# Moving tiles of a feed-forward stage read from the last column to the first, its weight words interleaved

## The chip, the cores and the metric

The kernel runs on one core of one Trainium2 chip. The metric is the device time of one execution in microseconds. Before the change it is 3116.07 us, the median of three runs (3114.22 to 3117.28).

## The reference

Two blocks stand one behind the other, all in float32. The first is a long convolution: a small network makes a filter of 12480 positions by 128 channels, and `u = x * v` (4 batches) is convolved with it by a Fourier transform of twice the length, then multiplied by `x`. The second is a feed-forward block on the 49920 tokens that come out of it:

```
u = x * v
y = np.fft.irfft(np.fft.rfft(u, n=L, axis=1) * Hf, n=L, axis=1)[:, :S, :]
x = (x * y).reshape(B * S, 128)
h = np.maximum(x @ w_in, 0.0)        # w_in: 128 x 2048
out = h * h @ w_out                  # w_out: 2048 x 128
```

## The kernel before

**The feed-forward part.** The tokens are cut into 98 column tiles (two of 446 columns, 50 of 512 and 46 of 510; `GN`). For each tile `i` and each of 8 pairs of hidden blocks `f`, `m_h` multiplies two 128x128 blocks of `w_in` with the tokens, `m_g` takes relu and square on ScalarE and VectorE, `m_l` makes the low word on VectorE, and `m_o` multiplies two 128x128 blocks of `w_out` with the result and adds it up over `f` in one PSUM bank. Every operand is kept as two float32r words, a high and a low one, and `mm3` makes one product of three matmuls: high weights by high moving tile (L95), low weights by the same high tile (L96), high weights by the low tile (L97). So one `f` is 12 matmuls, each with a weight load of its own, and the whole part has 98 x 8 x 12 = 9408 of them. Their moving operands are the tiles `zh`, `zl` (tokens) and `gh`, `gl` (hidden values).

**Where these tiles lie.** A weight tile `wt` holds 256 columns of both words, 2048 bytes in a partition: before, all 256 high words and then all 256 low words, so that the 128 words of one load are next to each other. The pools are filled from both ends of SBUF. Before, `zh`, `zl`, `gh` and `gl` of the pool `mp` begin at the same remainder of their address by 512 as the weight tiles (480). Once the convolution is done, `m_g` uses a second pool (`tp`, the name `tail`) for odd `f`; its tiles begin at remainder 128.

**The convolution** runs through four stages for each batch: `stage1` (L290 to L293), `stage2` (L380), `stage3` (L492) and `stage4`, whose matmuls are again three float32r ones by `mm3` (moving `ah`, `al` of 256 columns, stationary `tb` of 112). The other stages use plain float32 matmuls. In `stage3` the weights are every second word of the tile `v` (a step of 8 bytes). The order of all work is written out by hand: generators yield at three points, and the feed-forward loop calls `adv` to run the next piece of the next batch's convolution between its own matmuls. When all batches are through, the feed-forward part runs alone to the end.

Of the kernel before, what the change touches and what calls it, by code (L numbers as in the profile page):

```python
# [7 lines left out]
F32 = mybir.dt.float32  # L8
F32R = mybir.dt.float32r
# [8 lines left out]
I = 112  # L18
# [9 lines left out]
NS = NF // 2  # L28
# [10 lines left out]
TH = 4  # L39
CW = 256  # L40
NCW = DFF // CW


@with_exitstack
def hyena_moe_kernel(
# [34 lines left out]
    def pool(name, side="left", **kw):  # L80
        return tc.tile_pool(name=name, bufs=kw.pop("bufs", 2), side=side, reuse_waits="tile", **kw)
# [7 lines left out]
        for _ in range(k):  # L89
            nc.tensor.matmul(o[:, :128], zeros, zeros, start=True, stop=True)  # L90

    def mm3(o, L, R, first=True, last=True):
        lh, ll = L
        rh, rl = R
        nc.tensor.matmul(o, lh, rh, start=first, stop=False)  # L95
        nc.tensor.matmul(o, ll, rh, start=False, stop=False)  # L96
        nc.tensor.matmul(o, lh, rl, start=False, stop=last)  # L97
# [10 lines left out]
    def convert_weights(p, wp, raws, wt, chunks):  # L108
        V = nc.vector
        for c in chunks:  # L110
            low, high = raws[c][:, :, 0], raws[c][:, :, 1]
            mag, top, sgn = (p.tile([128, CW], I32, tag=k, name="cv") for k in ("cm", "ct", "cs"))
            mf = mag.bitcast(F32)
            tf = top.bitcast(F32)
            V.tensor_scalar(out=top, in0=high, scalar1=0x7FFFFFFF, scalar2=None, op0=ALU.bitwise_and)
            yield
            V.tensor_scalar(out=mf, in0=tf, scalar1=2.0**-15, scalar2=122880.0, op0=ALU.max, op1=ALU.min)
            yield
            V.tensor_scalar(out=top, in0=mag, scalar1=3, scalar2=0x7FFFFFFF, op0=ALU.logical_shift_left, op1=ALU.bitwise_and)
            yield  # L120
            V.tensor_scalar(out=mag, in0=low, scalar1=1, scalar2=None, op0=ALU.logical_shift_right)
            nc.gpsimd.tensor_copy(mf, mag)
            yield
            V.tensor_scalar(out=sgn, in0=high, scalar1=-0x80000000, scalar2=0x40000000, op0=ALU.bitwise_and, op1=ALU.bitwise_xor)
            yield
            V.tensor_tensor(out=top, in0=top, in1=sgn, op=ALU.bitwise_xor)
            wt[c] = wp.tile([128, 2, CW], F32R, tag="w", name="wt", bufs=2 * NCW)
            hi12, lo12 = wt[c][:, 0, :], wt[c][:, 1, :]
            nc.gpsimd.tensor_copy(hi12, tf)
            yield  # L130
            V.tensor_scalar(out=sgn, in0=top, scalar1=-0x800000, scalar2=None, op0=ALU.bitwise_and)
            yield
            V.scalar_tensor_tensor(out=mf, in0=mf, scalar=2.0**-51, in1=sgn.bitcast(F32), op0=ALU.mult, op1=ALU.mult)
            yield
            V.tensor_sub(out=tf, in0=tf, in1=hi12.bitcast(F32))
            yield
            V.tensor_add(out=lo12, in0=tf, in1=mf)
            yield
# [386 lines left out]
    def stage4(b, done, ring=None):  # L525
# [21 lines left out]
        with pool("s4") as p:  # L547
# [22 lines left out]
            def mm(t):  # L570
                if t >= NP:
                    return
                hi, lo = q.pop(t)
                tb = L.pop(t)
                A = bank()
                o = A[:I, :256]
                mm3(o, (tb[:, 0, :], tb[:, 2, :]), (hi[:, 0], lo[:, 0]), last=False)
                mm3(o, (tb[:, 1, :], tb[:, 3, :]), (hi[:, 1], lo[:, 1]), first=False)
                Y[t] = A

            def turn_first(t):

                zf = p.tile([I, 2 * D], F32, tag="zf", name="zf", bufs=1)
                nc.vector.tensor_mul(
                    out=zf.rearrange("p (c b i) -> p b c i", b=4, c=2),
                    in0=Y.pop(t)[:I, :256].rearrange("p (b i c) -> p b c i", b=4, c=2),
                    in1=X.pop(t).rearrange("p (b c i) -> p b c i", b=4, c=2),
                )
                o = bank()
                for c in range(2):  # L590
                    nc.tensor.transpose(o[:, c * I : (c + 1) * I], zf[:, c * D : (c + 1) * D], ident)
                idle(2)
                return o[:, 1 : 2 * I]
# [9 lines left out]
            def out_t(t):  # L603
                if t not in Y:
                    return
                xv = X.pop(t).rearrange("p (b c i) -> p b c i", b=4, c=2)
                zt = Z[t // 2 % 2]
                nc.vector.tensor_mul(
                    out=zt[:I].rearrange("p (b t c i) -> p t b c i", b=4, t=2, c=2)[:, t % 2],
                    in0=Y.pop(t)[:I, :256].rearrange("p (b i c) -> p b c i", b=4, c=2),  # L610
                    in1=xv,
                )
                if t % 2 == 0:
                    return
                zs = p.tile([128, 4 * D], F32, tag="zs", name="zs")
                nc.vector.transpose(out=zs, in_=zt)
                for k, w in enumerate(GW):
                    dst = zpart(b, t // 2, k).rearrange("(i b w) -> i b w", i=32, b=4)
                    src = zs[32 * k : 32 * k + 32]
                    if k == 0:  # L620
                        dst = dst.rearrange("i b (t w) -> i (b t) w", t=2)
                        src = src.rearrange("p (b t w) -> p (b t) w", b=4, t=2)[:, :, 1:]
                    elif k == 3:
                        dst = dst.rearrange("i b (q w) -> i (b q) w", q=4)
                        src = src.rearrange("p (b q w) -> p (b q) w", b=4, q=4)[:, :, :16]
                    else:
                        src = src.rearrange("p (b w) -> p b w", b=4)
                    nc.sync.dma_start(out=dst, in_=src)
                done[b] = t + 1
# [107 lines left out]
    wt = {}  # L737
# [13 lines left out]
    idle(20)  # L751
    held["tbb"].close()

    mp = ctx.enter_context(pool("mp", "right"))
    head = [mp.tile([D, GM], F32R, tag=k, name=k)[:, :GT] for k in ("zh", "zl")]
    s4 = stage4(0, done, take("t1p"))
# [1 line left out]
    idle(12)  # L758

    def wi(k, h, f):  # L760
        return wt[k * NCW + f // 2][:, h, f % 2 * 128 : (f % 2 + 1) * 128]

    def zload(i):
        zi = mp.tile([D, GM], F32, tag="zi", name="zi", bufs=1)[:, : GN[i]]
# [20 lines left out]
    def m_h(zT, f):  # L785
        A = psa.tile([128, 2, 512], F32, tag="A", name="A")
        for t in range(2):
            mm3(A[:, t, : zT[0].shape[1]], (wi(0, 0, 2 * f + t), wi(0, 1, 2 * f + t)), zT)
        return A

    def m_g(A, p, n, between, way):
# [31 lines left out]
    def m_o(i, f, hl):  # L823
        if f == 0:
            O[0] = bank() if tail and not nxt[0] else pso.tile([128, 512], F32, tag="O", name="O")
        o = O[0][:, : GN[i]]
        for t in range(2):
            mm3(o, (wi(1, 0, 2 * f + t), wi(1, 1, 2 * f + t)), (hl[0][:, t, :], hl[1][:, t, :]), first=(f == 0 and t == 0), last=(f == NS - 1 and t == 1))
        if f == NS - 1:
            return i, o  # L830
        return None

    def m_out(last):
        if last is not None:
            i, o = last
            ot = mp.tile([D, GM], F32, tag="ot", name="ot", bufs=1)[:, : GN[i]]
            nc.scalar.copy(ot, o)
            nc.sync.dma_start(out=out[:, GO[i] : GO[i] + GN[i]], in_=ot)
# [32 lines left out]
    for i in range(NM):  # L871
        for f in range(NS):
            adv(1)
            A = m_h(zT, f)
            last = m_o(*pend.pop(0)) if len(pend) > 1 else None
            adv(2)
            if not nxt[0] and not tail:
                tail.append(ctx.enter_context(pool("tp")))
            late.append((i, f, m_g(A, tail[0] if tail and f % 2 else mp, GN[i], lambda: m_out(last), way(i * NS + f))))
            while len(late) > len(tail):  # L880
                x, y, st = late.pop(0)
                pend.append((x, y, m_l(st, False)))
            if i + 1 < NM:
                if f == (1 if i else 3):
                    ready(i + 1)
                    zi = zload(i + 1)
                if f == (4 if i else 6):
                    nzT = zsplit(zi)
            adv(3)
            n = i * NS + f  # L890
            if stage[0] != since[0]:
                since = stage[0], n + 4
            owed += EXTRA[done[1] > 0]
            if owed >= 1 and stage[0] in (("s3", "s4") if done[1] else ("s2", "s3", "s4")) and nxt[0] == 1 and n >= since[1]:
                owed -= 1
                since = stage[0], n + 3
                for k in range(1, 4):
                    adv(k)
        if i + 1 < NM:
            zT = nzT  # L900
# [116 lines left out]
```

## Time and profile before

| what | value |
|---|---|
| median of three runs | 3116.07 us (3114.22 to 3117.28) |
| the profiled execution: span | 3112.0 us |
| TensorE matmul busy | 3072.7 us, 99% of the span |
| TensorE weight load busy | 2579.8 us, 83% |
| VectorE busy | 2538.0 us, 82% |
| ScalarE busy | 2419.1 us, 78% |
| GpSimd busy | 1501.6 us, 48% |

The span runs from the first to the last instruction of one profiled execution; the runs are timed without the profiler, around the whole execution, and their median stands 4.1 us above it. Matmuls are pipelined: the busy time of one contains the time in which its last columns leave the array, so that two successive ones overlap in the table. The pace is read from start to start.

### The profile page before, as it was taken

What the parts mean: (1) busy time and instruction counts of PE and PEld (TensorE: products, weight loads), DVE (VectorE), ACT (ScalarE), POOL (GpSimd) and SP (SyncE); (2) the same over time, 40 slices, a digit from 0 to 9 for tenths busy, and PEclk for the clock granted to TensorE, in tenths of its full rate; (3) what the DMA queues carried; (4) which work ended last, traced back from release to release, by engine and by line L of the source; (5) the groups of instructions that cost most, each with busy time, mean ns of one, the idle gap of its engine ahead of it and who ended that gap; (6) DMA issues with size and microseconds to landing.
All of it is one profiled execution on the core that took longest, in us unless ns stands there. A gap on an engine that the chain in (4) does not pass through costs nothing.

```text
span 3112.0 us, 49107 instructions
## 1 busy us (share of the span) xinstructions
PE 3072.7 (99%) x16086; PEld 2579.8 (83%) x16086; DVE 2538.0 (82%) x3080; ACT 2419.1 (78%) x3130; POOL 1501.6 (48%) x1631
## 2 busy tenths in 40 slices
PE   9989999999999999999999999999999999999999
PEld 7767888888888888888888888888888888888887
DVE  7888898878877988878877898878877799777776
ACT  5556777777788777788888877787788887878787
POOL 1249765556544565546644575646644466000000
PEclk9999999999999999999999999999999999999999
DMA  5783574434200664434300375434410176100000
GB/s 184 263 294 99 137 166 137 124 111 145 67 21 15 151 161 132 130 91 127 115 15 21 80 176 144 133 92 121 124 51 14 36 168 156 33 24 24 24 26 20
DMA packets 342623, 323.11 MB, mean 104 GB/s; under 512 B 161968, under 2 KB 288800, under 8 KB 342368
## 3 DMA queue, kind: packets, MB, share of 16 engines
q1 hardware_dynamic: 313216, 272.25, 30.2%
q0 software_dynamic: 29152, 47.72, 6.4%
q8 instruction: 128, 2.10, 0.3%
q14 instruction: 127, 1.04, 0.1%
HBM read 231.78 MB, written 65.60 MB: 96 GB/s over the span
## 4 chain that ended last, share of the span: by engine, by line
PE 92%; POOL 2%; DMA 2%; DVE 2%; issue 1%; ACT 1%; SPq 0%; DVEq 0%; ACTq 0%; POOLq 0%
PE A L95 11%; PE A L97 11%; PE A L96 11%; PE O L97 9%; PE O L96 9%; PE O L95 9%; PE F L380 6%; PE F L492 6%; PE F L293 5%; PE F L97 4%; PE F L95 4%; PE F L96 4%; PE A L290 2%; PE A L291 1%; POOL W L405 1%
## 5 line engine op out<-in xcount | busy, mean ns | idle before, releaser
L799 ACT ACTIVATE r<-A 128x1024 f32<-128x1024 f32 (+2 forms) x784 | 803.8, 1025 | 420.8 <-PE A L97 407.0
L818 DVE TENSOR_TENSOR gl<-r,gh 128x1020 fp32r<-128x1020 f32 (+1 forms) x433 | 642.5, 1484 | 113.9 <-ACT r L806 80.0
L95 PE MATMUL A<-zh,wt 128*128 128x512 f32 (+2 forms) x1568 | 671.4, 428 | 0.9 <-DVE gl L818 0.9
L97 PE MATMUL A<-zl,wt 128*128 128x512 f32 (+2 forms) x1568 | 613.8, 391 | 0.0
L96 PE MATMUL A<-zh,wt 128*128 128x512 f32 (+2 forms) x1568 | 612.9, 391 | 0.0
L802 ACT ACTIVATE gh<-r 128x1024 fp32r<-128x1024 f32 (+2 forms) x461 | 486.9, 1056 | 62.8 <-PE O L96 57.2
L97 PE MATMUL O<-gl,wt 128*128 128x512 f32 (+2 forms) x1248 | 487.4, 391 | 4.2 <-DVE gl L818 4.2
L96 PE MATMUL O<-gh,wt 128*128 128x512 f32 (+2 forms) x1248 | 485.0, 389 | 0.0
L95 PE MATMUL O<-gh,wt 128*128 128x512 f32 (+2 forms) x1248 | 484.9, 389 | 0.0
L804 DVE SCALAR_TENSOR_TENSOR A<-A,r 128x1024 f32<-128x1024 f32 (+2 forms) x350 | 425.4, 1215 | 68.1 <-ACT r L799 66.5
L818 DVE TENSOR_TENSOR gl<-A,gh 128x1024 fp32r<-128x1024 f32 (+2 forms) x350 | 426.1, 1218 | 63.1 <-ACT gh L802 20.4
L806 ACT ACTIVATE r<-r 128x1020 f32<-128x1020 f32 (+1 forms) x434 | 460.3, 1061 | 12.5
L813 DVE CAST gh<-r 128x1020 fp32r<-128x1020 f32 (+1 forms) x323 | 225.6, 698 | 221.2 <-ACT r L806 152.7
L782 POOL TENSOR_TENSOR zl<-zi,zh 128x512 fp32r<-128x512 f32 (+2 forms) x97 | 126.4, 1303 | 522.4 <-ACT zh L781 506.1
L567 POOL TENSOR_TENSOR al<-W,ah 112x512 fp32r<-112x512 f32 x214 | 281.9, 1318 | 189.2 <-ACT ah L561 185.0
L501 POOL TENSOR_TENSOR W<-c 112x224 f32<-112x224 f32 x256 | 217.6, 861 | 285.7 <-ACT c L499 275.0
L97 PEld LDWEIGHTS A<-zl,wt 128*128 128x128 f32 x1568 | 294.6, 188 | 64.7
L95 PEld LDWEIGHTS A<-zh,wt 128*128 128x128 f32 x1568 | 295.5, 188 | 51.4 <-DVE gl L818 3.1
L96 PEld LDWEIGHTS A<-zh,wt 128*128 128x128 f32 x1568 | 296.2, 189 | 45.1
L417 POOL TENSOR_TENSOR W<-W,m 112x256 f32<-112x256 f32 x168 | 177.8, 1058 | 247.3 <-DVE m L415 233.1
L97 PEld LDWEIGHTS O<-gl,wt 128*128 128x128 f32 x1248 | 234.2, 188 | 54.5 <-DVE gl L818 5.9
L96 PEld LDWEIGHTS O<-gh,wt 128*128 128x128 f32 x1248 | 234.2, 188 | 50.6
(127 smaller groups left out, 5495.3 us busy)
## 6 DMA issues: line engine op xcount, KB each, us to landing
ht<-Hd SPq DMA_DIRECT2D x224, 256.0 KB
tb<-t POOLq DMA_DIRECT2D x224, 196.0 KB, 3.1
xt<-x SPq DMA_DIRECT2D x224, 112.0 KB
xt<-xs SPq DMA_DIRECT2D x96, 224.0 KB
vt<-vs SPq DMA_DIRECT2D x96, 224.0 KB
tb<-t2s SPq DMA_DIRECT2D x168, 112.0 KB
Hd<-he SPq DMA_DIRECT2D x28, 512.0 KB
zd<-zs SPq DMA_DIRECT2D x222, 64.0 KB
```

What stands on the lines that cost most here:

```text
L95: nc.tensor.matmul(o, lh, rh, start=first, stop=False)
L96: nc.tensor.matmul(o, ll, rh, start=False, stop=False)
L97: nc.tensor.matmul(o, lh, rl, start=False, stop=last)
L380: nc.tensor.matmul(U[:I, k * 256 : (k + 1) * 256], tb[:KP, k, :], a[:, k], start=True, stop=True)
L501: nc.gpsimd.tensor_sub(out=dst[:, 1], in0=c[:, :, 0:3:2], in1=c[:, :, 3:0:-2])
L567: eng.tensor_sub(out=lo, in0=w, in1=hi.bitcast(F32))
L799: nc.scalar.activation(r, h, AF.Relu)
L802: nc.scalar.activation(hi, r, AF.Square)
L804: nc.vector.scalar_tensor_tensor(out=h, in0=h, scalar=0.0, in1=r, op0=ALU.max, op1=ALU.mult)
L806: nc.scalar.activation(r, r, AF.Square)
L813: nc.vector.tensor_copy(hi, g)
L818: nc.vector.tensor_sub(out=lo, in0=g, in1=hi.bitcast(F32))
```

## The change

Three things change, and no instruction moves: on each of the five queues the same instructions stand in the same order on the same operands' shapes. Buffers have other addresses, and four instructions (three of L799, one of L818) wait for other transfers, since a tile lies on other earlier tiles.

1. `mm3` gets a flag `back`, with which it reads both words of the moving tile from the last column to the first. The two calls of the feed-forward part and the two of `stage4` set it. In the feed-forward part the hidden values come out reversed and are reversed again by the second product, so the output has its old order; in `stage4` the VectorE multiplication that reads the PSUM bank (L584, L608) reads it from the end.
2. A weight tile holds high and low word of one column side by side: the 128 words of one load now stand 8 bytes apart, over 1024 bytes.
3. Two unused tiles, of 128 bytes (`gp`) ahead of the pool `mp` and of 224 bytes (`tp`) in the tail's pool, shift the tiles behind them. All of `zh`, `zl`, `gh`, `gl`, in either pool, now begin at remainder 352 by 512, and the weight tiles as before at 480.

```diff
+TP = 56
+MP = 32
...
-    def mm3(o, L, R, first=True, last=True):
+    def mm3(o, L, R, first=True, last=True, back=False):
         lh, ll = L
-        rh, rl = R
+        rh, rl = (x[:, ::-1] for x in R) if back else R
...
-            wt[c] = wp.tile([128, 2, CW], F32R, tag="w", name="wt", bufs=2 * NCW)
-            hi12, lo12 = wt[c][:, 0, :], wt[c][:, 1, :]
+            wt[c] = wp.tile([128, CW, 2], F32R, tag="w", name="wt", bufs=2 * NCW)
+            hi12, lo12 = wt[c][:, :, 0], wt[c][:, :, 1]
...
-                mm3(o, (tb[:, 0, :], tb[:, 2, :]), (hi[:, 0], lo[:, 0]), last=False)
-                mm3(o, (tb[:, 1, :], tb[:, 3, :]), (hi[:, 1], lo[:, 1]), first=False)
+                words = [[x[:, a].rearrange("p d c -> p (d c)") for x in (hi, lo)] for a in range(2)]
+                mm3(o, (tb[:, 0, :], tb[:, 2, :]), words[0], last=False, back=True)
+                mm3(o, (tb[:, 1, :], tb[:, 3, :]), words[1], first=False, back=True)
...
-                    in0=Y.pop(t)[:I, :256].rearrange("p (b i c) -> p b c i", b=4, c=2),
+                    in0=Y.pop(t)[:I, 255::-1].rearrange("p (b i c) -> p b c i", b=4, c=2),
...
+    ctx.enter_context(pool("gp", "right")).tile([128, MP], F32, name="gp", bufs=1)
     mp = ctx.enter_context(pool("mp", "right"))
...
-        return wt[k * NCW + f // 2][:, h, f % 2 * 128 : (f % 2 + 1) * 128]
+        return wt[k * NCW + f // 2][:, f % 2 * 128 : (f % 2 + 1) * 128, h]
...
-            mm3(A[:, t, : zT[0].shape[1]], (wi(0, 0, 2 * f + t), wi(0, 1, 2 * f + t)), zT)
+            mm3(A[:, t, : zT[0].shape[1]], (wi(0, 0, 2 * f + t), wi(0, 1, 2 * f + t)), zT, back=True)
...
-            mm3(o, (wi(1, 0, 2 * f + t), wi(1, 1, 2 * f + t)), (hl[0][:, t, :], hl[1][:, t, :]), first=(f == 0 and t == 0), last=(f == NS - 1 and t == 1))
+            mm3(o, (wi(1, 0, 2 * f + t), wi(1, 1, 2 * f + t)), (hl[0][:, t, :], hl[1][:, t, :]), first=(f == 0 and t == 0), last=(f == NS - 1 and t == 1), back=True)
...
                 tail.append(ctx.enter_context(pool("tp")))
+                tail[0].tile([128, TP], F32, tag="tp", name="tp", bufs=1)
```

## Rows read from the trace of the kernel before

**Rows 1.** The page: span, busy time by engine, TensorE's granted clock in 40 slices.

```profile
span 3112.0 us, 49107 instructions
...
PE 3072.7 (99%) x16086; PEld 2579.8 (83%) x16086; DVE 2538.0 (82%) x3080; ACT 2419.1 (78%) x3130; POOL 1501.6 (48%) x1631
...
PEclk9999999999999999999999999999999999999999
```

**Rows 2.** The page: the chain that ended last, shares of the span by engine.

```profile
PE 92%; POOL 2%; DMA 2%; DVE 2%; issue 1%; ACT 1%; SPq 0%; DVEq 0%; ACTq 0%; POOLq 0%
```

**Rows 3.** Busy time by stretch: PE, PEld, DVE, ACT, POOL (instructions), clock, DMA share, GB/s.

```profile
1000.00:1200.00 200.00, 198.79 (x1041) 168.73 (x1040) 178.81 (x208) 157.74 (x188) 108.20 (x125) 1.00 0.59 141
...
2700.00:2800.00 100.00, 100.00 (x439) 82.07 (x438) 74.03 (x74) 79.61 (x82) 6.47 (x5) 1.00 0.09 24
```

**Rows 4.** Timeline of the tail: start us, length us, engine, line, operation.

```profile
2900.59 0.40 PE L95 MATMUL F<-gh,wt 128*128 128x510 f32 x1
2900.59 0.19 PEld L96 LDWEIGHTS F<-gh,wt 128*128 128x128 f32 x1
...
2901.99 0.39 PE L95 MATMUL A<-zh,wt 128*128 128x510 f32 x1
...
2903.36 0.39 PE L95 MATMUL F<-gh,wt 128*128 128x510 f32 x1
...
2904.72 0.39 PE L95 MATMUL A<-zh,wt 128*128 128x510 f32 x1
```

**Rows 5.** Groups of PE matmuls by form: count, busy us, mean ns, idle before.

```profile
L97 PE MATMUL A<-zl,wt 128*128 128x512 f32 x800 | 315.5, 394 | 0.0
L96 PE MATMUL A<-zh,wt 128*128 128x512 f32 x800 | 313.9, 392 | 0.0
L97 PE MATMUL O<-gl,wt 128*128 128x512 f32 x800 | 313.4, 392 | 4.2 <-DVE gl L818 4.2
...
L95 PE MATMUL O<-gh,wt 128*128 128x512 f32 x800 | 311.7, 390 | 0.0
...
L96 PE MATMUL A<-zh,wt 128*128 128x510 f32 x736 | 287.4, 390 | 0.0
...
L380 PE MATMUL F<-W,tb 120*112 120x256 f32 x672 | 170.2, 378 | 0.0
...
L95 PE MATMUL O<-gh,wt 128*128 128x510 f32 x416 | 161.5, 388 | 0.0
...
L95 PE MATMUL F<-ah,tb 112*112 112x256 f32 x448 | 125.4, 280 | 0.4 <-ACT ah L561 0.4
...
L97 PE MATMUL F<-gl,wt 128*128 128x510 f32 x320 | 125.4, 392 | 0.0
...
L96 PE MATMUL A<-zh,wt 128*128 128x446 f32 x32 | 11.6, 364 | 0.0
```

**Rows 6.** A piece of the chain in order of time: start us, length us, what.

```profile
659.91 1.73 PE F L380 x8
```

**Rows 7.** Groups of weight loads by form: count, busy us, mean ns, idle before.

```profile
L96 PEld LDWEIGHTS A<-zh,wt 128*128 128x128 f32 x1568 | 296.2, 189 | 45.1
...
L492 PEld LDWEIGHTS F<-ft,v 112*112 112x112 f32 x1792 | 209.0, 182 | 19.0 <-POOL v L479 5.3 <-DVE W L500 1.1
...
L380 PEld LDWEIGHTS F<-W,tb 120*112 120x112 f32 x672 | 117.8, 175 | 29.5
```

**Rows 8.** The tile `wt`: ns min/median/max of one group, first and last start us.

```profile
L129 POOL CAST wt<-cv x16: 466/522/524, 88.9 to 151.0; 128x256 fp32r<-128x256 f32 x16
```

**Rows 9.** Groups of VectorE's instructions: count, busy us, mean ns, idle before.

```profile
L608 DVE TENSOR_TENSOR z<-F,xt 112x256 f32<-112x256 f32 x222 | 90.5, 410 | 7.2 <-DMA xt<-x 7.2
...
L137 DVE TENSOR_TENSOR wt<-cv 128x256 fp32r<-128x256 f32 x16 | 6.8, 424 | 0.5
...
L117 DVE TENSOR_SCALAR cv<-cv 128x256 f32<-128x256 f32 x16 | 4.7, 294 | 0.6
...
L115 DVE TENSOR_SCALAR cv<-raw 128x256 int32<-128x256 int32 x16 | 4.6, 286 | 0.0
```

More of the change, by code (lines that the diff above doesn't have):

```diff
@@ L609, in out_t @@
                     out=zt[:I].rearrange("p (b t c i) -> p t b c i", b=4, t=2, c=2)[:, t % 2],
-                    in0=Y.pop(t)[:I, :256].rearrange("p (b i c) -> p b c i", b=4, c=2),
+                    in0=Y.pop(t)[:I, 255::-1].rearrange("p (b i c) -> p b c i", b=4, c=2),
                     in1=xv,
```

## The prediction

> **What bounds the kernel now.** The page comes first. TensorE is busy for 99% of the span, the others for 48 to 83%, and the granted clock is at nine tenths or more in every slice [rows 1], that is, at 2.4 GHz, the higher of its two levels, nearly throughout. The chain that ended last is TensorE for 92% [rows 2]. So what a matmul costs is what the kernel costs, and the question is whether a matmul takes longer than its columns need.
>
> The table by stretch gives the pace. Between 2700 and 2800 us the feed-forward part runs alone: 439 matmuls of 510 columns in 100 us, 227.8 ns from start to start, with no gap [rows 3]. At 2.4 GHz 510 columns, one in each clock, are 212.5 ns, so 15.3 ns go elsewhere. A matmul of the same kernel that loses almost nothing is that of `stage2`: 8 follow each other in 1.73 us, 216.3 ns each [rows 6], for 256 columns. It is plain float32, two clocks to a column, so 512 clocks or 213.3 ns, and only 3 ns more. The two differ by some 12.4 ns (216.3 less two clocks is 215.4). The groups by form say the same of the whole run: 378 ns for the 512 clocks of L380, against 390 to 394 ns for the 512 clocks of L95 to L97 [rows 5].
>
> The timeline of the tail shows that this surplus hangs on where the tile lies. Six matmuls from `gh` and `gl`, of one shape, with weights from the same tiles, take 1.40 us (2900.59 to 2901.99) and some microseconds later 1.36 us (2903.36 to 2904.72) [rows 4]. The two sixes differ in the pool from which `gh` and `gl` come: the first has odd `f` (the tail's pool, remainder 128), the second even `f` (remainder 480, as the weights). The rows also show what runs beside a matmul: the weight load of the next one starts with it (2900.59 both) and lasts 0.19 us. I read the surplus as stalls in which the moving read and the weight read want the same part of SBUF. That is an inference: the trace shows that the cost depends on the tile's place, not which part of the memory was asked for.
>
> Against this reading stands the Trainium skill, TensorE: Matmul & The Clock Gate, section "Step-by-step: what each phase is for": TensorE has two independent SBUF read ports, and loading the next weights takes nothing from the running matmul. By that rule there is nothing to gain, the term below is 0 and the time 3116 us. The 1.40 against 1.36 us do not fit it, but they alone do not name the weight load.
>
> **The change part by part.** *The meeting of the two reads.* A load of 128 columns takes 189 ns, one of 112 takes 175 [rows 7]: 14 ns for 16 columns, 0.88 ns or about two clocks a column; 128 columns are read in about 110 ns, the first half of a matmul. So before, the moving read goes 4 bytes on in each clock and the weight read 4 bytes in two clocks; they pass each other again and again. After, the weight words are 8 bytes apart, 4 bytes a clock on average: both walk at one pace. If the array takes its weights from the last column to the first (no row shows this), both also walk the same way, and keep the distance with which they begin; the moving tiles' remainder 352 and the weights' 480 set it to 128 bytes. Two reads at one pace cannot run into each other again once they are apart, so I expect nearly all of the surplus to go.
>
> Its size, by lengths against 378 ns for 512 clocks (377 for 510, 350 for 446) [rows 5]. L96 of the same form as a shown L95 lies within 2 ns, and L95 of `A`, whose mean holds the switch from float32 matmuls ahead of it, is taken as L96. 512 columns: 2400 into `A` at 393 ns, 15 over, 36.0 us; 2400 into `O` at 391, 13 over, 31.2. 510 columns: 2208 into `A` at 390, 13 over, 28.7; 1248 into `O` at 389, 12 over, 15.0; 960 into `F` at 392, 15 over, 14.4. 446 columns: 192 at 364, 14 over, 2.7. Together 128 us. By the pace of the tail it is 9408 x 12.4 = 117 us. I take 122 us, and leave a tenth of it, 12 us, to first meetings: **110 us gained**. Bounds: 128 us gained, and, with stalls doubled because weight reads now touch twice the memory, 122 us lost.
>
> *`stage4`.* 1344 matmuls of 256 columns, 280 ns at 378 - 256 / 2.4 = 271 [rows 5], 9 over: 12 us in all. Only the direction changes here; the weights stay 4 bytes apart, so the paces still differ. Between 12 us gained and 12 lost, I take **6 us gained**, since reads that walk the same way meet less often.
>
> *Loads from every second word.* L492 loads every second word already: 182 ns for 112 columns against 175 for L380's adjacent ones [rows 7]. With 7 ns more the new load takes 196 ns and is hidden under the matmul of 215 ns. Twice the reading time would not be hidden (189 + 110 = 299 ns a matmul, 9408 x 71 = 670 us more), but L492 is far from that. I take 0.
>
> *Reading a tile backwards.* No row of TensorE has a negative step, so its own price is not shown; the pace of two clocks a column of L380 [rows 5, 6] would be its worst, and nothing its best. I take nothing: the same words are read, in the other order. VectorE's 222 instructions of L608 [rows 9] read their bank backwards at the same distance of two words as before. I take 0 there too; 10% more would be 9 us, hidden on an engine that is busy for 82% [rows 1].
>
> *Writing the weights.* 16 casts of 522 ns on GpSimd [rows 8] and 16 results of 424 ns on VectorE [rows 9] now write every second word. Twice as long would be 15 us, around 90 to 155 us and partly on the path. Reading every second word costs VectorE nothing: L115 does in 286 ns what L117 does from adjacent words in 294 [rows 9]. I take 0 by this, and the range has room for the other end.
>
> *What is late next.* With TensorE some 4 to 5% faster, VectorE rises from 178.81 of 200 us to about 94% between 1000 and 1200 us [rows 3], a `stage4` stretch; those last about 600 us in all. It remains below 100%, but the queues are in order and TensorE will wait for `gl` now and then (4.2 us in all before, at L97 [rows 5]). 4% of 600 us is 24 us between nothing and all given back; I take half, **12 us lost**. In the tail VectorE (74%) and ScalarE (80%) have room [rows 3].
>
> Sum: 110 + 6 - 12 = 104 us. The profiled span is 3112.0 us, which gives 3008, and the median stands 4.1 us above the span: **3012 us**.
>
> **The rivals.** *Some of the surplus stays* (14 in 100). The distance of 128 bytes is not enough, or part of the surplus is no stall but belongs to the float32r form: between the two sixes lie only 6 ns a matmul, not 12. Half of the 122 us gained gives 3055; by how much stays, 3046 to 3100 and a little above.
>
> *Nothing happens* (7 in 100). The whole surplus belongs to float32r, and only the tail's odd tiles gain what the even ones have: some 640 matmuls at 6 ns, 4 us, 3112. This is also what the rule of the Trainium skill's TensorE page, cited above, would lead to.
>
> *The reads meet more* (16 in 100). If the array takes its weights from the first column on, both reads walked the same way before, 2 bytes apart in a clock; the reversed moving read would now come towards the weight read, 8 bytes in a clock, over weights of 1024 bytes instead of 512. For it speaks that no row tells which way a load walks; against it, that the surplus of L380, where both reads have one pace, is 3 ns. If the stalls double, 9408 matmuls lose another 13 ns, 122 us, and the time is 3238. From a mean of 228 ns from start to start on, the change loses.
>
> *My case* (63 in 100): 2975 to 3046 us. All stalls gone in both parts and nothing given back is 128 + 12 = 140 us, 2976.
>
> **The numbers.** The likeliest case gives 3012. With the second case down to 3100 the range holds some 77 to 80 in 100, so it goes from 2972 to 3100. Within 0.2% (6 us) is about what a measurement of this kernel cannot tell from no change. Faster by more: 0.63 + 0.14 = 0.77; the same 0.07; slower 0.16.
>
> **What would show it.** Right: in the tail the pace is 215 to 217 ns, some 462 matmuls in 100 us instead of 439; L95 to L97 of 512 columns last 378 to 382 ns in either pool; the loads stay below 200 ns; VectorE's share rises to 94% in the `stage4` stretches, with some microseconds of waits of TensorE for `gl`. Wrong: a pace near 221 ns (half stays), 228 (nothing), over 228 (they meet more), or a load of 215 ns and more, at which the weights become the bound.

## The result, and the profile after

The changed kernel takes 3154.18 us (median of 4 runs, 3153.52 to 3155.91), the kernel before in the same comparison 3115.39 us (4 runs, 3114.22 to 3117.28). The ratio is 1.0124, with a 95% interval from 1.0110 to 1.0139: 1.2% slower, where 3012 us had been forecast, and above the range's 3100.

The page of the changed kernel, its span and the busy time by engine, which answers to [rows 1], and its chain, which answers to [rows 2]:

```profile
span 3152.7 us, 49110 instructions
...
PE 3116.9 (99%) x16086; PEld 2634.8 (84%) x16086; DVE 2534.4 (80%) x3080; ACT 2419.3 (77%) x3130; POOL 1518.2 (48%) x1631
...
PE 92%; DVE 2%; DMA 2%; POOL 2%; issue 1%; ACT 1%; SPq 1%; DVEq 0%; ACTq 0%; POOLq 0%
```

The span is 40.7 us longer (3152.7 against 3112.0), and TensorE's busy time grew by 44.2 us (3116.9 against 3072.7). The same 16086 matmuls run and the same engine sets the end; each matmul costs more. VectorE's busy time, which was to be the next limit, is 3.6 us shorter.

Busy time by stretch, as in [rows 3]:

```profile
1000.00:1200.00 200.00, 199.23 (x1041) 171.65 (x1040) 176.33 (x205) 158.09 (x190) 111.93 (x124) 1.00 0.57 137
2700.00:2800.00 100.00, 100.00 (x430) 82.70 (x430) 71.41 (x72) 78.64 (x82) 5.13 (x4) 1.00 0.08 24
```

430 matmuls in 100 us instead of 439. These counts also hold the matmuls that reach over an edge of the stretch, so that 100 us divided by them is a nanosecond too little; by the starts alone, a matmul follows the last after 233.3 ns against 228.9 before. That is 4.5 ns more, and for 9408 feed-forward matmuls 42 us, close to the 40.7 us by which the span grew. The granted clock is 1.00 in both stretches before and after, so it is not the clock. For the matmuls of 512 columns the starts before lay 229.3 ns apart and lie 233.4 ns apart now, 4.1 ns more.

Timeline of the tail, as in [rows 4]: start, length, engine, line, operation. Two sixes from `gh` and `gl`, one from each pool, and where each ends.

```profile
2900.95 0.40 PE L97 MATMUL F<-gh,wt 128*128 128x510 f32 x1
...
2902.35 0.40 PE L97 MATMUL A<-zh,wt 128*128 128x510 f32 x1
...
2903.75 0.40 PE L97 MATMUL F<-gh,wt 128*128 128x510 f32 x1
...
2905.15 0.40 PE L97 MATMUL A<-zh,wt 128*128 128x510 f32 x1
```

Both take 1.40 us now (2900.95 to 2902.35, 2903.75 to 2905.15). Before, one took 1.40 and the other 1.36. The two pools have become equal, but at the slower value; and it is not the shift of the tiles that makes them equal, as the reversed reading alone does it too (`back_only`, below).

Groups of PE matmuls by form, as in [rows 5] (the lines moved down by two):

```profile
L99 PE MATMUL O<-gl,wt 128*128 128x512 f32 x800 | 318.4, 398 | 4.5 <-DVE gl L822 4.5
L98 PE MATMUL A<-zh,wt 128*128 128x512 f32 x800 | 317.8, 397 | 0.0
...
L98 PE MATMUL A<-zh,wt 128*128 128x510 f32 x736 | 292.3, 397 | 0.0
...
L382 PE MATMUL F<-W,tb 120*112 120x256 f32 x672 | 171.7, 381 | 0.0
...
L97 PE MATMUL O<-gh,wt 128*128 128x510 f32 x416 | 165.2, 397 | 0.0
...
L97 PE MATMUL F<-ah,tb 112*112 112x256 f32 x448 | 126.8, 283 | 0.4 <-ACT ah L563 0.4
...
L98 PE MATMUL A<-zh,wt 128*128 128x446 f32 x32 | 12.2, 380 | 0.0
```

The lengths are uniform: 397 or 398 ns for 510 and 512 columns, wherever the operand lies and whichever word of the weights is loaded, where there had been 388 to 394 (446 columns: 380 against 364). Left aside is L97 into `A`, whose mean holds the switch from other matmuls. A length is longer than the step from start to start (397 ns against 233), and the lengths rise by more than the pace; the pace is what adds up. L382, plain float32 and untouched by the change, stays where it was within 3 ns (381 against 378).

Weight loads, VectorE's groups and the casts into `wt`, as in [rows 7 to 9], each from its own view:

```profile
L98 PEld LDWEIGHTS A<-zh,wt 128*128 128x128 f32 x1568 | 305.7, 195 | 42.1
```

```profile
L611 DVE TENSOR_TENSOR z<-F,xt 112x256 f32<-112x256 f32 x222 | 90.4, 410 | 6.6 <-DMA xt<-x 6.6
...
L139 DVE TENSOR_TENSOR wt<-cv 128x256 fp32r<-128x256 f32 x16 | 6.8, 425 | 0.5
```

```profile
L131 POOL CAST wt<-cv x16: 486/545/568, 88.8 to 147.9; 128x256 fp32r<-128x256 f32 x16
```

The loads from every second word take 195 ns instead of 189 and remain under the matmul. Reading a PSUM bank backwards costs VectorE nothing (410 ns both). The casts take 23 ns more each by their medians, 0.4 us in all.

### The profile page after: what moved, and what is told of

The parts are those of the page before. It is cut to its first block, busy times and chain, and to the rows that moved or that the text cites. A ratio compares the mean times of both kernels' runs of the same rounds, so it can differ in the third digit from the quotient of the medians.

```text
span 3152.7 us, 49110 instructions
## 1 busy us (share of the span) xinstructions
PE 3116.9 (99%) x16086; PEld 2634.8 (84%) x16086; DVE 2534.4 (80%) x3080; ACT 2419.3 (77%) x3130; POOL 1518.2 (48%) x1631
## 4 chain that ended last, share of the span: by engine, by line
PE 92%; DVE 2%; DMA 2%; POOL 2%; issue 1%; ACT 1%; SPq 1%; DVEq 0%; ACTq 0%; POOLq 0%
PE A L97 11%; PE A L98 11%; PE A L99 11%; PE O L99 9%; PE O L97 9%; PE O L98 9%; PE F L382 6%; PE F L494 5%; PE F L295 5%; PE F L97 4%; PE F L99 4%; PE F L98 4%; PE A L292 3%; DMA Hd<-he 1%; DMA ht<-Hd 1%
## 5 line engine op out<-in xcount | busy, mean ns | idle before, releaser
L822 DVE TENSOR_TENSOR gl<-r,gh 128x1020 fp32r<-128x1020 f32 (+1 forms) x433 | 635.2, 1467 | 115.0 <-ACT r L810 79.1
L97 PE MATMUL A<-zh,wt 128*128 128x512 f32 (+2 forms) x1568 | 680.7, 434 | 0.9 <-DVE gl L822 0.8
L98 PE MATMUL A<-zh,wt 128*128 128x512 f32 (+2 forms) x1568 | 622.3, 397 | 0.0
L99 PE MATMUL A<-zl,wt 128*128 128x512 f32 (+2 forms) x1568 | 622.1, 397 | 0.0
L99 PE MATMUL O<-gl,wt 128*128 128x512 f32 (+2 forms) x1248 | 495.7, 397 | 4.5 <-DVE gl L822 4.5
L97 PE MATMUL O<-gh,wt 128*128 128x512 f32 (+2 forms) x1248 | 495.0, 397 | 0.0
L98 PE MATMUL O<-gh,wt 128*128 128x512 f32 (+2 forms) x1248 | 494.8, 397 | 0.0
L503 POOL TENSOR_TENSOR W<-c 112x224 f32<-112x224 f32 x256 | 232.5, 922 | 280.4 <-ACT c L501 270.6
L99 PEld LDWEIGHTS A<-zl,wt 128*128 128x128 f32 x1568 | 303.8, 194 | 60.7
L97 PEld LDWEIGHTS A<-zh,wt 128*128 128x128 f32 x1568 | 305.1, 195 | 48.4 <-DVE gl L822 2.4
L98 PEld LDWEIGHTS A<-zh,wt 128*128 128x128 f32 x1568 | 305.7, 195 | 42.1
L99 PEld LDWEIGHTS O<-gl,wt 128*128 128x128 f32 x1248 | 241.8, 194 | 55.9 <-DVE gl L822 7.4
L98 PEld LDWEIGHTS O<-gh,wt 128*128 128x128 f32 x1248 | 241.9, 194 | 48.7
```

What stands on the lines that cost most here:

```text
L503: nc.gpsimd.tensor_sub(out=dst[:, 1], in0=c[:, :, 0:3:2], in1=c[:, :, 3:0:-2])
L822: nc.vector.tensor_sub(out=lo, in0=g, in1=hi.bitcast(F32))
```

## The experiments

The theories: the surplus over the columns' clocks comes from the weight read meeting the moving read (the prediction's); it belongs to the moving read of float32r itself, by the place of the tile and its direction; or other engines' accesses to SBUF make it.

**One part alone.** The reversed reading alone, in the feed-forward part and in `stage4`:

```diff
-        rh, rl = R
+        rh, rl = (x[:, ::-1] for x in R) if back else R
```

> Only the reversed reading of the moving tiles; weights and places of the tiles as before. Three theories of the 1.2% lost. Direction (the array takes its weights from the first column, so the reversed read comes towards them): the tail's pace rises from 227.8 to 233 ns or more here already, about 3155 us. Interleaving (a load that touches twice the memory stalls the moving read more, whatever its direction): the pace stays at 227 to 229 ns, about 3116 us. Place (only the remainder 352 is bad): also 227 to 229 ns here.

Measured: 3151.81 us, ratio 1.0125 (1.0095 to 1.0154). The stretch in the tail:

```profile
2800.00:2900.00 100.00, 100.00 (x431) 80.55 (x430) 72.21 (x72) 77.97 (x80) 5.86 (x5) 1.00 0.08 24
```

The whole loss is there with this part alone: 431 matmuls in 100 us, 233 ns in either pool, although the weights lie as before.

The side-by-side words alone, read forwards:

```diff
-            wt[c] = wp.tile([128, 2, CW], F32R, tag="w", name="wt", bufs=2 * NCW)
+            wt[c] = wp.tile([128, CW, 2], F32R, tag="w", name="wt", bufs=2 * NCW)
```

> Only the weight words side by side; moving tiles read forwards, at their old places. Interleaving: the pace is 233 ns, as in the whole change, about 3155 us. Direction: two forward reads at one pace keep apart, 215 to 220 ns, about 3020 us. Place: 227 to 229 ns, 3116 us.

Measured: 3152.97 us, ratio 1.0128 (1.0099 to 1.0158); 233 ns from start to start in the mean, single ones between 227 and 240.

```profile
2800.00:2900.00 100.00, 100.00 (x429) 83.28 (x429) 72.38 (x72) 78.34 (x80) 6.40 (x5) 1.00 0.09 24
```

The two unused tiles alone:

```diff
+    ctx.enter_context(pool("gp", "right")).tile([128, MP], F32, name="gp", bufs=1)
...
+                tail[0].tile([128, TP], F32, tag="tp", name="tp", bufs=1)
```

> Only the two unused tiles, so that all moving tiles begin at remainder 352 by 512. Place: the pace is 233 to 235 ns in both pools, about 3155 us. Interleaving and direction: some value between the 225 and 235 ns that the single matmuls of before show at their remainders, with both pools alike, about 3100 to 3140 us.

Measured: 3130.73 us, ratio 1.0056 (1.0034 to 1.0079). The tail is a little faster than before (443 in 100 us, against 439; 226.7 ns from start to start in both pools), the matmuls of 512 columns ahead of it slower (232.4 ns from start to start, against 229.3):

```profile
2800.00:2900.00 100.00, 100.00 (x443) 82.79 (x442) 74.38 (x74) 81.08 (x84) 6.48 (x5) 1.00 0.09 26
```

The change without the tiles that shift:

```diff
-    ctx.enter_context(pool("gp", "right")).tile([128, MP], F32, name="gp", bufs=1)
...
-                tail[0].tile([128, TP], F32, tag="tp", name="tp", bufs=1)
```

> Reversed reading and weight words side by side, without the two unused tiles, so that the pool mp begins at the weights' own remainder 480 and the tail's pool at 128. Place: the pace of even f in the tail differs from 233 ns and is lower, about 220 ns, and the time falls below 3116 us. Interleaving: 233 ns whatever the place. Direction: 233 ns or a little beside it, since two reads that come towards each other meet wherever they begin.

Measured: 3155.44 us, ratio 1.0136 (1.0107 to 1.0166), 233 ns in both pools.

What follows from the four: every part loses by itself, and the losses do not add up (1.25 + 1.28 + 0.56% alone, 1.24% together). With the reversed reading the pace is some 233 ns in the three kernels that have it, whatever the weights' step and the tiles' place: once it is there, the other parts add nothing.

**Is it the weight read?** The middle matmul of each three gets 64 weight columns instead of 128, so that its load, which runs beside the first matmul, reads half as much. (This leaves the low weight words' share out of half of the outputs.) In the kernel before:

```diff
-        nc.tensor.matmul(o, ll, rh, start=False, stop=False)
+        nc.tensor.matmul(o[:64] if half else o, ll[:, :64] if half else ll, rh, start=False, stop=False)
```

> The kernel before, with 64 instead of 128 weight columns in the middle matmul of each feed-forward product (the low weights): the low-word correction is left out for half of the outputs. The middle load is half as long; it runs during the first matmul of the three. Theory A, the surplus is the moving read stalled by the weight read: the first matmul's pace falls by about half of its surplus, from 228 to about 222 ns, the other two stay at 228. Theory B, the surplus belongs to the moving read itself (so much for each column): all three stay at 226 to 230 ns.

Measured: 3112.69 us in one run (before on this chip 3115.07). Groups of the stretch from 2700 to 3050 us:

```profile
L96 PE MATMUL A<-zh,wt 128*64 128x510 f32 x256 | 100.0, 391 | 0.0
...
L95 PE MATMUL A<-zh,wt 128*128 128x510 f32 x256 | 99.6, 389 | 0.0
```

The first matmul of each three, beside the short load, is followed by the next after 227.5 ns (into `A`) and 227.1 (into `F`), against 227.9 and 229.0 before; the 222 ns of the theory of stalls do not come. Timeline of this run: a six from `gh` and `gl` of odd `f` (the tail's pool), where it ends, one of even `f`, and where it ends.

```profile
2900.20 0.39 PE L95 MATMUL F<-gh,wt 128*128 128x510 f32 x1
...
2901.59 0.39 PE L95 MATMUL A<-zh,wt 128*128 128x510 f32 x1
...
2902.96 0.39 PE L95 MATMUL F<-gh,wt 128*128 128x510 f32 x1
...
2904.32 0.39 PE L95 MATMUL A<-zh,wt 128*128 128x510 f32 x1
```

The six of even `f` takes 1.36 us, as before [rows 4]; that of odd `f` takes 1.39 instead of 1.40 (over the tail from 2700 to 3050 us, 230.1 ns a matmul instead of 232.9). So where the tiles lie well the shorter load changes nothing, and where they lie badly it gives back some 3 of the 6 ns by which that place is slower. The weight read has a share in the spread by place, and none that shows in the rest.

The same edit in the changed kernel, with a load of 64 columns:

> The same cut (low weights of 64 columns in the middle matmul) in the changed kernel. Theory A: the first matmul of the three falls from 233 to about 224 ns, the other two stay at 233. Theory B: all three stay at 233 ns.

Measured: 3158.88 us in one run. In the same stretch:

```profile
L98 PEld LDWEIGHTS A<-zh,wt 128*64 128x64 f32 x250 | 34.0, 136 | 10.0
...
L97 PE MATMUL A<-zh,wt 128*128 128x510 f32 x251 | 99.6, 397 | 0.0
```

The load is down from 193 to 136 ns, and the matmul beside it keeps its 397 ns and its 233 ns from start to start. In the changed kernel no stall goes where the weight read is over sooner: for the greater part of the surplus the reading of the prediction has lost its cause.

**Is it the place?** In the kernel before, the moving tiles are shifted by 0 to 480 bytes in steps of 32, another step for each column tile. The shift of `zh`, and of `gh` and `gl` alike:

```diff
-        hi = mp.tile([D, GM], F32R, tag="zh", name="zh")[:, :n]
+        j = 8 * (j % 16)
+        hi = mp.tile([D, GM + SL], F32R, tag="zh", name="zh")[:, j : j + n]
```

> The kernel before, but the moving tiles of each column tile begin 0, 32, ... 480 bytes further on, in turn with the column tile's number, so that one run shows the pace at 16 places of the tiles against the weights (adjacent words, forward reading). Theory A: the pace runs through 215 to 235 ns with the place, with a period. Theory B: it does not hang on the place by more than the 7 ns seen so far (226 to 233), and no place comes near 216.

Measured: 3126.46 us. Grouped by the step of the column tile, 510 columns have 228 to 232 ns and 512 columns 230 to 233.

The same with the words of the weights side by side:

```diff
-        return wt[k * NCW + f // 2][:, h, f % 2 * 128 : (f % 2 + 1) * 128]
+        return wt[k * NCW + f // 2][:, f % 2 * 128 : (f % 2 + 1) * 128, h]
```

> The same scan of 16 places with the weight words side by side and forward reading: both reads at one pace, the same way if the array takes its weights from the first column. Theory A with that order of loading: most places at 216 to 220 ns and some that are bad at 235 to 240. Theory A with the other order: no place below 225, since the reads come towards each other. Theory B: 230 to 235 ns at every place.

Measured: 3137.43 us, 230 to 233 ns at all places. So the place shifts the pace by 3 to 4 ns, and no place comes near the 215.4 ns on which the forecast was built.

**Matmuls alone.** Rows of 16 equal matmuls are put behind the end of the kernel before, where no other engine works (their results go nowhere). Four of them:

```diff
+            nc.tensor.matmul(o[:, :n], V, M[:, 32 : 32 + n], start=True, stop=True)
...
+            nc.tensor.matmul(o[:, :n], V, M[:, 32 : 32 + n][:, ::-1], start=True, stop=True)
...
+        nc.tensor.matmul(o[:, :256], V.bitcast(F32), M[:, 32:288].bitcast(F32), start=True, stop=True)
...
+        nc.tensor.matmul(o, V, M[:, 32:1056:2], start=True, stop=True)
```

> The kernel before, and at its end, with nothing else running, rows of 16 equal matmuls each: one to eight times 64 columns forwards and backwards, 384 columns at 16 places 32 bytes apart in both directions, 512 columns with 32, 64 and 128 weight columns, with adjacent weights or every second word, plain float32, and a moving tile of every second word. Theory B (the surplus belongs to the float32r moving read, so much for each stretch of columns): backwards about 35 cycles of 1.2 GHz for each 64 columns, that is 29.2 ns each and 233 ns for 512, at every place and with 32 weight columns as with 128; forwards 225 to 235 ns; plain float32 of 256 columns 216 ns in either direction. Theory C (the surplus comes from other engines' use of SBUF): 215 to 217 ns for 512 columns in either direction here. Theory A, for what is left of it: with 32 weight columns below 220 ns.

The kernel with its rows took 3292.7 us. Groups of the appended stretch:

```profile
L954 PE MATMUL F<-M,wt 128*128 128x512 f32 x16 | 7.6, 662 | 0.0
...
L948 PE MATMUL F<-M,wt 128*128 128x256 f32 x32 | 7.1, 379 | 0.0
...
L939 PE MATMUL F<-M,wt 128*32 128x512 f32 x16 | 3.9, 396 | 0.0
...
L919 PE MATMUL F<-M,wt 128*128 128x512 f32 x16 | 3.9, 396 | 0.0
L923 PE MATMUL F<-M,wt 128*128 128x512 f32 x16 | 3.9, 398 | 0.0
...
L923 PE MATMUL F<-M,wt 128*128 128x256 f32 x16 | 3.6, 415 | 0.0
...
L919 PE MATMUL F<-M,wt 128*128 128x256 f32 x16 | 2.1, 281 | 0.0
```

L919 reads 512 columns forwards and L923 backwards, with nothing beside them on the core but the next weight load: 233 ns from start to start for both. L939 does it backwards with 32 weight columns: 233 too. The surplus is there in full, so the other engines do not make it. L948 is plain float32, of which the profile shows two records for each matmul (32 for 16): (7.1 - 0.379) / 31 = 217 ns for 256 columns in one record, the floor that the prediction took, of another data type.

One group misses the 29.2 ns for each 64 columns that were expected backwards: 256 columns take 3.6 us for 16 (217 ns from start to start) against 2.1 forwards (118), and 192 columns 216 ns against 114, while from 320 columns on the directions differ by some 2 ns at most. Why is open; `stage4` also reads 256 columns backwards, with 112 weight columns, and there it does not happen (119 ns).

**The better place for the kernel before.** Its tail pool gets 352 unused bytes, so that all moving tiles have the weights' remainder, 480:

```diff
+                tail[0].tile([128, 88], F32, tag="tp", name="tp", bufs=1)
```

> The kernel before, with 352 unused bytes ahead of the tail's pool alone, so that its tiles too begin at remainder 480, as the pool mp's do; everything forwards, weights adjacent. If the place of the moving tile alone sets the forward pace, the odd f of the tail go from 233 to 227 ns: some 640 matmuls gain 6 ns each, 4 us, and the time is about 3111 us, 0.1% faster than before. If not, 3115 us.

Measured: 3109.8 us (10 runs) against 3114.09 (13 runs), ratio 0.9986 (0.9976 to 0.9995): 4.3 us faster than the kernel before, and so faster than both.

```profile
2800.00:2900.00 100.00, 100.00 (x442) 82.61 (x442) 74.40 (x74) 81.20 (x84) 6.48 (x5) 1.00 0.09 25
```

442 in 100 us instead of 439, and every six takes 1.36 us: what one of the two pools of the tail had before [rows 4], both have now.

**Place and step of the weights, alone.** Rows of 12 matmuls of 510 columns behind the kernel before, for 4 places of the weights by 8 of the moving tile, with weights adjacent and in every second word, forwards and backwards:

```diff
+                nc.tensor.matmul(o[:, :510], Q[:, q : q + 128], M[:, a : a + 510], start=True, stop=True)
...
+                nc.tensor.matmul(o[:, :510], Q[:, q : q + 256 : 2], M[:, a : a + 510][:, ::-1], start=True, stop=True)
```

> The kernel before, and at its end, alone on the core, rows of 12 equal matmuls of 510 float32r columns: 8 places of the moving tile (32 bytes apart, by 256) by 4 places of the weights (0, 32, 128, 224), each with adjacent weight words and with every second word, forwards and backwards. If the weight read stalls the moving read (theory A), the forward rows with adjacent words run through 216 to 235 ns with the distance of the two places. If a float32r column costs what it costs (theory B), backwards 232 to 234 ns in every row, whatever the weights' step; forwards 225 to 235 ns by the moving tile's place alone, the same for all four places of the weights. If the step of the weights matters by itself, the forward rows with every second word stand at 233 ns and those with adjacent words below.

Measured (the whole took 3469.71 us): forwards, the distance of the two places by 256 bytes counts, moving less weights; for the four places of the weights it gives nearly the same values, so it is not the moving tile's place alone. ns from start to start in a row of 12, lowest and highest of the four (without the first row of all, which holds one pause of 110 ns):

```
bytes of distance            0        32       64       96       128      160      192      224
forwards, adjacent weights   227      227-229  231      233      231-233  233      229-235  232-233
forwards, every second word  233      234-236  230-233  230      227      230      230      235
backwards, either            233-234 at every place
```

The 229 at a distance of 192 is one row of four; the others have 235.

Timeline: twelve forwards with adjacent weights at a distance of 0, twelve at 192, and twelve backwards.

```profile
3134.81 2.89 PE L916 MATMUL F<-M,Q 128*128 128x510 f32 x12
...
3151.39 2.98 PE L916 MATMUL F<-M,Q 128*128 128x510 f32 x12
...
3304.30 2.97 PE L926 MATMUL F<-M,Q 128*128 128x510 f32 x12
```

The first row less one matmul of 388 ns is 2.50 us for 11 starts, 227 ns. The kernel before reads forwards, with adjacent weights at a distance of 0: it stood at the best of these places already, but for the odd tiles of its tail (128 less 480 is 160 by 256: 233 ns here, the six of 1.40 us there). The changed kernel has a distance of 128 with every second word, which is the best place of that layout as well, but only forwards.

**The change without the reversal.** If so, the change read forwards should be as fast as before:

```diff
-        rh, rl = (x[:, ::-1] for x in R) if back else R
+        rh, rl = R
```

> The whole change without the reversed reading: weight words side by side and all moving tiles at remainder 352, 128 bytes from the weights' by 256. In the rows alone on the core this distance is the best one for forward reading with every second weight word, 272.4 cycles of 1.2 GHz or 227 ns for 510 columns, against 226.6 for the distance 0 with adjacent words that the kernel before has. If those rows carry over, the tail's pace is 227 ns in both pools, and the 512-column tiles lie at 227 to 229 ns too: 3095 to 3112 us, no slower than before, and the reversed reading alone is what loses 1.2%. If the interleaved words cost something of their own in the kernel, the pace is 233 ns and the time 3150 us.

Measured: 3137.21 us (5 runs, before 3116.3), ratio 1.0068 (1.0055 to 1.0082).

```profile
2800.00:2900.00 100.00, 100.00 (x433) 84.39 (x432) 73.44 (x73) 79.11 (x82) 6.46 (x5) 1.00 0.08 24
```

232 ns from start to start in the tail, between the two cases of the expectation (227 and 233). Even without the reversal the change loses 0.7%, with the words side by side at the best place that the rows alone had shown for them; the reversal on top of it brings the loss to 1.24%, some 0.6% more.

**Load length, and the data type, alone.** Rows of 96 matmuls of 510 columns over the 8 places: float32r with 128, 64 and 32 weight columns, 32 backwards, then bfloat16 in both directions:

```diff
+            nc.tensor.matmul(o[:32, :510], Q[:, 32:64], M[:, a : a + 510], start=True, stop=True)
...
+            nc.tensor.matmul(o[:, :510], QB[:, 32:160], MB[:, a : a + 510], start=True, stop=True)
```

> The kernel before, and at its end, alone on the core, rows of 12 equal matmuls of 510 columns at 8 places of the moving tile, forwards with float32r words and 128, 64 and 32 weight columns, backwards with 32, and with bfloat16 words forwards and backwards with 128. If the spread by place (226 to 236 ns with 128 columns) is the weight read's doing, it shrinks with the load, and the floor shows: 215 ns if all of the surplus is the weight read's, 225 ns if some 11 ns belong to float32r itself. If the load's length changes neither, the place counts by the start of the two reads alone. Backwards with 32: 233 ns if the reversed reading has a pace of its own. bfloat16: 215 ns in both directions if the surplus comes from 4-byte words at full rate; about 225 forwards and 233 backwards if it is every moving read's.

The whole took 3242.8 us. Timeline of the rows:

```profile
3109.74 22.50 PE L918 MATMUL F<-M,Q 128*128 128x510 f32 x96 [0.30 <-DVE Q L914]
3132.08 22.21 PE L922 MATMUL F<-M,Q 128*64 128x510 f32 x96
3154.13 22.21 PE L926 MATMUL F<-M,Q 128*32 128x510 f32 x96
3176.18 22.59 PE L930 MATMUL F<-M,Q 128*32 128x510 f32 x96
3198.61 20.81 PE L934 MATMUL F<-MB,QB 128*128 128x510 bf16 x96
3219.26 20.80 PE L938 MATMUL F<-MB,QB 128*128 128x510 bf16 x96
```

The distance of two starts, divided by 96, is the pace: 232.7, 229.7, 229.7 and 233.6 ns for float32r, and (3219.26 - 3198.61) / 96 = 215.1 for bfloat16, with the same 215 backwards. Loads of 188, 135 and 109 ns gain 3 ns at most, and by place the row with 32 columns still has 227 to 235. (The first row holds one start that comes 340 ns after the last; without it, it has 231.5.) With two bytes to the element in both operands the surplus is gone, with the same number of columns, instructions and weight columns. So it belongs to the float32r matmul itself. That within it the moving read is to blame is argued from its dependence on direction and place, not shown apart.

## Why the prediction was wrong

**What bounds the kernel**: right. TensorE is the path before and after, and 4.5 ns more for each of 9408 matmuls, 42 us, came out as 40.7 us more of span. The 227.8 ns that it read from the count [rows 3] are 228.9 by the starts, so that its 12.4 ns over the floor would have been 13.5: no cause of the miss.

**"The meeting of the two reads"** is the step that failed, and with it the 110 us. It had two parts. The floor of 215.4 ns was taken from L380 [rows 6], plain float32; a float32r row of 510 columns never came below 226.5 ns in the mean in any run here, with or without other work beside it. And the surplus over that floor was read as stalls by the weight read, from the one sign that it hangs on the place of the tile. That sign was true (1.36 and 1.40 us, and 227 to 236 ns by distance), but it accounts for at most 9 ns above the 226.6 of the best place, half a load gave back some 3 of the 6 at a bad one, and the kernel before already had the best distance nearly everywhere. The 11 ns below 226.6 are no stall of that kind: neither half nor a quarter of the load lifts them, and only another data type did.

**Two costs taken at nothing** make the loss. *"Reading a tile backwards"*: backwards, float32r runs at some 233.3 ns at every place tried; against the 227.7 to 229.3 ns that groups of 510 and 512 columns had before, 4 to 6 ns for 9408 matmuls make up the loss of some 40 us, and this part alone lost as much (`back_only`). The prediction had noted that no row shows a negative step and had given it bounds, but put none of that into the sum or a rival. *The words side by side* were priced by the load alone ("Loads from every second word", "Writing the weights"). Those prices were right (196 ns expected, 195 measured, hidden; 0.4 us for the casts), but the pace of the matmul itself rose: read forwards, the kernel still loses 0.7% with them at their best place, and 1.28% at the old places. So without the reversal the forecast would have been wrong as well.

**`stage4`**: 6 us gained expected. The groups of `ah` rose from 280 to 283 ns (126.8 us against 125.4 for 448), and by the starts of its 1344 matmuls `stage4` lost about 1 us. That the reversed reading is the reason is not shown apart.

**"What is late next", 12 us lost**: no occasion. VectorE has 176.33 of 200 us in the stretch from 1000 us instead of 94%, and TensorE waits for `gl` 4.5 us at L99 against 4.2 [rows 5].

**The rivals.** *The reads meet more* had the sign and the point from which it decides (over 228 ns), but by luck: not the mechanism, since shorter loads change little and nothing at all in the changed kernel, and not the size (3238). *Nothing happens* had the nature of the surplus, that most of it belongs to float32r. Its small term, 4 us for the odd tiles of the tail, came out as 4.3 us once they were shifted alone. The Trainium skill, TensorE: Matmul & The Clock Gate, speaks of this at two places. The rule of two independent read ports, in "Step-by-step: what each phase is for", was weighed against [rows 4] and set aside; where the tiles lie well the runs with short loads agree with it (1.36 us for a six with half the load and with all of it), while at the worse place half the load gave back some 3 ns and the distance to the weights moves the pace by up to 9. The Trainium skill's section "Wait — 56ns, not 53.3ns?" of the same page gives columns by 2.4 GHz plus some 2.5 ns, an estimate of 215.0 for 510: the bfloat16 rows agree (215.1), the float32r rows do not (227 to 236).

**Still open.** Why every second word at its best distance gives 232 ns in the kernel and 227 in the rows alone; why the tail with the two unused tiles alone ran at 226.7 ns, at a distance where the rows alone have 231 to 233; what in the memory makes the reversed read the same at every place; and whether the 11 ns that float32r has over bfloat16 come from the width of its words or from its arithmetic. In the rows the same weights are loaded each time and in the kernel others, which was not taken apart.

## What to carry to other kernels

Take the floor of an operation from rows of the same data type and access, and where none exists, put a row of it alone behind the end of a kernel before building on an inferred mechanism: two such rows would have shown 233 ns in either direction. A dependence on a tile's place shows that place matters, not that the best place lies far below what is there. Put a price on every access that no row shows, also where the same words are read in another order; here two such terms at nothing were the loss. With float32r moving tiles of adjacent words, read forwards and try the distance to adjacent weights in the kernel itself: a multiple of 256 bytes was the best in the rows alone and was worth 0.14% in the tail, but 128 bytes did as well there and was slower ahead of it.

## What the runs showed of the hardware

- Backwards, the cost of float32r goes with the columns from 320 on: in the rows alone 147 ns for 320, 204 for 448 and 233 for 512, that is 0.46 ns a column, 1.09 to 1.10 clocks at 2.4 GHz. At 192 and 256 columns it does not: 216 and 217 ns, against 114 and 118 forwards.
- bfloat16 has the same 215 ns for 510 columns in both directions.
- A float32r moving tile of every second word runs at half the rate: 16 matmuls of 512 columns took 7.6 us (L954), against 3.9 us from adjacent words (L919).
- For a weight load the step costs little: 195 ns against 189 for 128 columns, while 64 columns take 135 and 32 take 109 ns.
